# The first fourteen loads in a fixed order, the key-value matrix times WO as three products of rounded parts and rests, and a new order table

## The chip, the cores and the metric

The kernel runs on one core of a Trainium2 chip. Its time is the device time of one execution in microseconds (us); the number that counts is the median of the timed runs. The engines are named as in the profile: PE is the matrix engine (PEld its weight loads), DVE the vector engine, ACT the scalar engine, POOL the general engine; SP issues most of the transfers.

## The reference, cut to what matters

One sequence of S = 2048 rows with D = 512 columns, all in 32-bit floating point. Two branches share a layer norm.

```
xn = layernorm(x)
q, k, v = (xn @ wqkv), 32 heads of 16 columns
pq, pk = phi(q), phi(k)            # phi(t) = t+1 or exp(t), plus 1e-6
kv  = sum over rows of pk (x) v    # 16x16 per head
z   = sum over rows of pk
s   = (pq @ kv) / (pq . z + 1e-6)  # per head
s   = s @ wo
g   = silu(mixer_and_mlp(xn))      # w1, shift by rows, w2; then w3 (512x1376), gelu, w4
out = x + s * g
```

The kernel does not form v. It gathers G = xn^T pk (512x512) over the rows, multiplies it with the value weights WV, keeps the 16x16 blocks on the diagonal (a mask), and has the masked key-value matrix `kvt`. Then M = kvt times WO, a 512x512 matrix, so that s is one product of the scaled queries with M. The step "kvt times WO" is one of the places that the change touches.

## The kernel before, in words

**Arithmetic.** Most products are done with operands in a rounded 32-bit form (type fp32r in the profile) that PE streams faster than full 32-bit operands. To keep the precision, each operand is split into a rounded part `hi` (ACT, a copy into an fp32r tile, line 168) and a rest `lo` (DVE, a subtraction, line 191), and a product is the sum of three matmuls, hi*hi, hi*lo and lo*hi (`products`, which issues them through `mm`, line 146; `rounded` and `split` make the parts). A few products are done with the full 32-bit operands instead (`slow=True`); such a matmul stands in the trace as two records.

**Stages.** (1) Start: the key weights `wk_s0` to `wk_s3` (256 KB each, one per 128 input columns) and the transposed rows `xt0_0` to `xt0_3` of the first quarter of the sequence (each loaded as two halves of 128 KB) come in; PE multiplies chunk by chunk into four banks `k`. For chunk 0 it multiplies the raw operands, for chunks 1 to 3 the split ones, so ACT makes `wk_1h`, `u_1h`, `wk_2h` and so on, and DVE the rests `wk_1l`, `u_1l`. (2) Keys, queries and the G sums for all 16 row tiles, with weights for later stages being prepared beside. (3) The first mixer stage (`mix1`, `forms`, `mix2`) for four quarters, in four blocks of the Strassen-Winograd kind with seven products instead of eight (`seven`). In this stage, between quarters 2 and 3, stand the steps that the change touches: `kv` (32 records), the mask (`kvt`), then `m` (kvt times WO) and the copies into the tiles `mq`. (4) The MLP up and down projections with the attention products (`forms_m` makes further sums of the `mq` tiles for it) between them. (5) A last stretch of down projections, gates and stores.

**Order.** The program is not run in the order in which it is written. Every step is first recorded by `Plan.add` (line 96) with the engine, an assumed duration and the steps that it depends on. `deadlines` (line 243) walks the PE steps in their written order and gives each a nominal time; every other step gets a due time, worked back from its first user (`backward`, line 264). `nudged` (line 237) then changes due times by a table `SOONER` of pairs (number of the step, quarter microseconds earlier, negative for later). `emit` (line 270) runs a model of the engines: at each point it takes, among the steps of an engine that could start about then, the one that is due first (line 340), and issues it. So each engine's queue is a fixed sequence in the program, decided when it is built; on the chip the engines wait for each other by semaphores. A step that writes a tile also needs a free buffer of its pool (90 buffers of the tag `p` hold most of the tiles; `emit`, lines 311 to 327). For SP's transfers the model holds at most eight in flight (line 303).

The lines around the product with WO are these (1705 to 1719):

```
    kvt = piece("kvt")
    MQ = [[piece(f"mq{h}{d}") for d in range(2)] for h in range(2)]
    for gg in range(NC):
        cs = gg * P, (gg + 1) * P
        ps = bank(f"kv{gg}").cols(0, P)
        for c in range(NC):
            pl.mm(ps, WV.raw[c].cols(*cs), gs[c].cols(*cs), c == 0, c == NC - 1, slow=True)
        pl.tt(kvt.cols(*cs), ps, bmask, ALU.mult)
    forms(b)
    mix2(QT + 1)
    for gg in range(NC):
        ps = bank(f"m{gg}")
        pl.mm(ps, kvt.cols(gg * P, (gg + 1) * P), WO.raw[gg], True, True, slow=True)
        for d in range(2):
            pl.act(MQ[gg // 2][d].cols(gg % 2 * TH, (gg % 2 + 1) * TH), ps.cols(d * TH, (d + 1) * TH), AF.Copy)
```

`Weights` loads a matrix in four pieces `raw[c]`; its method `split` makes a rounded part (ACT, 128x512) and a rest (DVE, 128x512) of each; `chunk(c)` gives such a pair. Before, WO is loaded and used raw, and `split` is never called for it.

Of the kernel before, what the change touches and what calls it, by code (L numbers as in the profile page):

```python
# [14 lines left out]
P = 128  # L15
# [65 lines left out]
class Op:  # L81
    __slots__ = ("eng", "busy", "lat", "emit", "pre", "post", "tiles", "opens", "two", "table", "patience", "soon", "loads",
                 "nom", "due", "ready", "at", "end", "mb", "order")


class Plan:
# [9 lines left out]
    def add(self, eng, busy, lat, reads, writes, emit, two=False, table=None, mb=0.0):  # L96
        op = Op()
        op.eng, op.busy, op.lat, op.emit, op.two, op.table, op.mb = eng, busy, lat, emit, two, table, mb
        op.pre, op.post, op.tiles, op.opens = {}, [], {}, False
        op.order = len(self.ops)  # L100
# [142 lines left out]
    def deadlines(self, first):  # L243
# [18 lines left out]
        self.backward()  # L262

# [133 lines left out]
def linear_attn_gated_by_mixer(  # L397
# [55 lines left out]
    def rounds(name):  # L453

        return piece(name + "h", F32R), piece(name + "l", F32R)
# [1254 lines left out]
        for c in range(NC):  # L1710
            pl.mm(ps, WV.raw[c].cols(*cs), gs[c].cols(*cs), c == 0, c == NC - 1, slow=True)
        pl.tt(kvt.cols(*cs), ps, bmask, ALU.mult)
    forms(b)
    mix2(QT + 1)
    for gg in range(NC):
        ps = bank(f"m{gg}")
        pl.mm(ps, kvt.cols(gg * P, (gg + 1) * P), WO.raw[gg], True, True, slow=True)
        for d in range(2):
            pl.act(MQ[gg // 2][d].cols(gg % 2 * TH, (gg % 2 + 1) * TH), ps.cols(d * TH, (d + 1) * TH), AF.Copy)
# [76 lines left out]
    for b in LINE:  # L1796
# [10 lines left out]

    SOONER = (
# [103 lines left out]
```

## Time and profile before

| | |
|---|---|
| median of 3 timed runs | 502.96 us (502.81, 502.96, 505.84) |
| the profiled execution | 505.87 us |
| its span, first to last instruction | 504.2 us |
| left outside the span | 1.67 us |
| mean granted clock of PE | 0.995 |

The span is read by engine, by stage and by wait. "Busy" of PE is the time in which at least one matmul is under way; matmuls overlap in the pipeline, so what one costs is read from the distance between starts, or between ends, of neighbours, and not from its own duration. In the timeline a row gives start, duration, engine, line, what is written from what, the shape, how many such records are merged, and in brackets the idle time of the engine before it with what ended the wait. "SPq" rows are the issues of transfers. The granted clock is 1.00 when PE has its full clock.

### The profile page before, as it was taken

The page shows a single profiled execution, that of the slowest core. Times are in us where ns is not written, and L with a number is a line of the kernel's source. Part 1 is how long each engine was busy: PE and PEld are TensorE (multiplying, and loading weights), DVE is VectorE, ACT ScalarE, POOL GpSimd, SP SyncE. Part 2 cuts the span into 40 slices and gives each one's busy share as a digit, 9 for nine tenths or more (in the row PEclk, how much of TensorE's full clock was granted, in tenths as well). Part 3 has the DMA queues.
Part 4 walks back from the last instruction along what each step waited for, and adds up shares of the span by engine and source line. Part 5 has one row for each costly group of instructions (what it writes and reads, how often), then busy time and mean ns, then how long its engine had stood idle before and what let it go on. Part 6 is the DMA issues. An engine that isn't in the chain of part 4 may idle for free. (4 is left out here: it accounts for less than half of the span.)

```text
span 504.2 us, 9867 instructions
## 1 busy us (share of the span) xinstructions
PE 494.8 (98%) x3240; PEld 446.5 (89%) x3240; DVE 437.8 (87%) x889; ACT 373.2 (74%) x840; POOL 121.2 (24%) x194
## 2 busy tenths in 40 slices
PE   7999999999999999999999999999999999999896
PEld 4787878888888998899988999999999999999896
DVE  4898997798989958899999999999999799795773
ACT  4798999867687779999988667765766776664631
POOL 1167322447941312133100021100000000234220
PEclk9999999999999999999999999999999999999999
DMA  7949895989995899999987499695444799599995
GB/s 212 317 129 237 231 249 175 210 229 326 316 293 121 228 300 253 278 218 271 347 281 207 148 229 276 185 324 166 136 126 126 216 317 359 128 211 285 296 200 165
DMA packets 87082, 117.44 MB, mean 233 GB/s; under 512 B 10328, under 2 KB 39160, under 8 KB 87032
## 3 DMA queue, kind: packets, MB, share of 16 engines
q1 hardware_dynamic: 75512, 96.11, 58.9%
q0 software_dynamic: 11520, 20.71, 24.8%
q8 instruction: 25, 0.41, 0.3%
q14 instruction: 25, 0.20, 0.1%
HBM read 72.66 MB, written 39.93 MB: 223 GB/s over the span
## 5 line engine op out<-in xcount | busy, mean ns | idle before, releaser
L225 POOL DMA_DIRECT2D xo<-x1d x12 | 11.6, 987 | 158.5 <-ACT d_a121h L168 106.5
L225 POOL DMA_DIRECT2D th<-in_x x14 | 12.1, 885 | 50.0 <-DVE th L201 19.0
L598 POOL TENSOR_TENSOR rs<-w,nhalf 128x4 f32<-128x4 f32 (+2 forms) x10 | 12.4, 1239 | 49.0 <-DVE w L196 35.5
L225 POOL DMA_DIRECT2D o<-xnd x16 | 14.0, 915 | 35.2 <-ACT o L168 15.5
L168 ACT ACTIVATE th<-xo 128x512 f32<-128x512 f32 (+1 forms) x16 | 9.7, 612 | 13.3 <-DVE xo L201 10.8
L225 POOL DMA_DIRECT2D zacc<-ke x12 | 12.0, 1002 | 27.2 <-DMA zacc<-ke 19.7
L225 POOL DMA_DIRECT2D xt<-nrow x16 | 15.2, 1297 | 11.7 <-DMA nrow<-ar 5.8
L191 DVE TENSOR_TENSOR ht<-h,abc 128x512 f32<-128x512 f32 x16 | 11.0, 688 | 5.8 <-PE h L146 5.7
L168 ACT ACTIVATE p<-pe 128x256 f32<-128x256 f32 x20 | 7.6, 382 | 8.0 <-PE pe L146 7.9
L168 ACT ACTIVATE ht<-ht 128x512 f32<-128x512 f32 x16 | 9.8, 624 | 4.1 <-DVE ht L191 4.0
L168 ACT ACTIVATE u<-pb 128x256 f32<-128x256 f32 x20 | 7.6, 381 | 5.9 <-PE pb L146 5.6
L168 ACT ACTIVATE y<-o,nm,rs 128x512 f32<-128x512 f32 x16 | 11.9, 805 | 0.0
L168 ACT ACTIVATE sq<-o,mv 128x512 f32<-128x512 f32 x16 | 11.5, 722 | 0.2
L201 DVE SCALAR_TENSOR_TENSOR pq<-pq,rd 128x512 f32<-128x512 f32 x16 | 10.9, 684 | 0.2
L201 DVE SCALAR_TENSOR_TENSOR qz<-pq,zb 128x512 f32<-128x512 f32 x16 | 10.9, 680 | 0.0
L1456 DVE TENSOR_REDUCE den<-qz 128x32 f32<-128x512 f32 x16 | 10.7, 672 | 0.1
L168 ACT ACTIVATE p<-pb 128x256 f32<-128x256 f32 x20 | 7.6, 382 | 4.2 <-PE pb L146 3.9
L168 ACT ACTIVATE sq<-o 128x512 f32<-128x512 f32 x16 | 10.0, 629 | 0.6 <-PE h L146 0.6
L168 ACT ACTIVATE x<-x,nm,rs 128x512 f32<-128x512 f32 x12 | 9.3, 803 | 0.0
L201 DVE SCALAR_TENSOR_TENSOR th<-th,so 128x512 f32<-128x512 f32 x12 | 8.2, 680 | 0.8 <-ACT th L168 0.7
L168 ACT ACTIVATE sq<-x,mv 128x512 f32<-128x512 f32 x12 | 8.6, 715 | 0.1
L168 ACT ACTIVATE den<-den 128x32 f32<-128x32 f32 x16 | 3.4, 224 | 6.1 <-DVE den L1456 6.0
(2043 smaller groups left out, 2436.2 us busy)
## 6 DMA issues: line engine op xcount, KB each, us to landing
w_s<-in_w SPq DMA_DIRECT2D x28, 256.0 KB, 5.3
x<-in_x SPq DMA_DIRECT2D x16, 256.0 KB, 5.8
xt<-in_xt SPq DMA_DIRECT2D x16, 256.0 KB, 5.1
xnd<-x SPq DMA_DIRECT2D x16, 256.0 KB, 7.0
xt<-nrow POOLq DMA_DIRECT2D x16, 256.0 KB, 7.0
pqd<-qr SPq DMA_DIRECT2D x16, 256.0 KB, 3.2
o<-xnd POOLq DMA_DIRECT2D x16, 256.0 KB, 6.4
x1d<-o SPq DMA_DIRECT2D x16, 256.0 KB
```

The costliest lines, as they stand in the source:

```text
L168: nc.scalar.activation(out.get(), src.get(), func, scale=get(scale), **kw)
L191: self.vec(eng, out, [a, b], lambda: self.e(eng).tensor_tensor(out.get(), a.get(), b.get(), op=op), True)
L201: lambda: self.nc.vector.scalar_tensor_tensor(out.get(), a.get(), get(s), b.get(), op0=op0, op1=op1),
L225: lambda: self.nc.gpsimd.dma_start(out.get(), get(src), accum_op=ALU.add), mb=mb)
L598: lambda: g.tensor_tensor(out.get(), src.get(), nh.get(), op=ALU.pow))
L1456: pl.add("DVE", .6, .68, [t], [den], lambda: nc.vector.tensor_reduce(den.get(), t.get().rearrange("p (h d) -> p h d", d=DH), axis=AX.X, op ...
```

## The change: a fixed turn, split operands for M, a new table

1. A new method `in_turn` gives fourteen loads a rank in the order of a list. In `deadlines` a ranked step gets the due time 20 times its rank less 600 us, far before everything else, so that SP issues these fourteen first and in that order. The list alternates weights and rows from the first load on: key weights chunk 0 (first half), rows chunk 0 (first half of the rows), weights chunk 0 (second half), rows chunk 0 (second half), then weights and rows (first halves) of chunk 1, of chunk 2, of chunk 3, then `x0`, then the second halves of the rows of chunks 1, 2, 3.
2. `kvt` is split (`rounded(*kvr, kvt)`), WO is split (`WO.split()`), and kvt times WO is done as three fp32r matmuls for each of the four blocks instead of one full 32-bit matmul.
3. The table `SOONER` is another one: 625 pairs in place of 622. The numbers of the steps behind the new ones move, so the pairs can't be compared one by one.

```diff
         self.backward()
+        for op in self.ops:
+            if op.rank is not None:
+                op.due = 20.0 * op.rank - 600.0
+
+    def in_turn(self, names):
+
+        ranks = {}
+        for n, name in enumerate(names):
+            ranks.setdefault(name, []).append(n)
+        for op in self.ops:
+            if op.eng == "SP" and op.mb:
+                r = ranks.get(next(iter(op.tiles)).name)
+                if r:
+                    op.rank = r.pop(0)
...
         pl.tt(kvt.cols(*cs), ps, bmask, ALU.mult)
+    kvr = rounds("kvr")
+    rounded(*kvr, kvt)
+    WO.split()
     forms(b)
     mix2(QT + 1)
     for gg in range(NC):
         ps = bank(f"m{gg}")
-        pl.mm(ps, kvt.cols(gg * P, (gg + 1) * P), WO.raw[gg], True, True, slow=True)
+        products(ps, [both(kvr, gg * P, (gg + 1) * P) + WO.chunk(gg)])
...
+    pl.in_turn(["wk_s0", "xt0_0", "wk_s0", "xt0_0", "wk_s1", "xt0_1", "wk_s2", "xt0_2", "wk_s3", "xt0_3", "x0", "xt0_1",
+                "xt0_2", "xt0_3"])
     SOONER = (
-        15, 75, 17, -32, 23, 4, 27, 4, 31, 4, 39, 3, 45, 46, 47, -6, 48, -56, 62, 6, 81, 2, 106, -37, 110, -38,
+        25, -4, 31, 6, 40, 6, 47, -61, 48, -65, 72, 6, 76, 9, 81, 11, 82, 3, 83, 5, 92, -48, 94, 13, 95, -14,
...
     )
```

More of the change, by code (lines that the diff above doesn't have):

```diff
@@ L82 @@
     __slots__ = ("eng", "busy", "lat", "emit", "pre", "post", "tiles", "opens", "two", "table", "patience", "soon", "loads",
-                 "nom", "due", "ready", "at", "end", "mb", "order")
+                 "nom", "due", "ready", "at", "end", "mb", "order", "rank")
 class Plan:
@@ L99, in add @@
         op.pre, op.post, op.tiles, op.opens = {}, [], {}, False
-        op.order = len(self.ops)
+        op.order, op.rank = len(self.ops), None
         op.patience, op.soon = self.patience, False
```

120 rows, old and new, of the table SOONER are left out of this document.

## The prediction

> **What bounds the kernel now.** I read the page first, for the engines' shares.
>
> ```profile
> span 504.2 us, 9867 instructions
> PE 494.8 (98%) x3240; PEld 446.5 (89%) x3240; DVE 437.8 (87%) x889; ACT 373.2 (74%) x840; POOL 121.2 (24%) x194
> ```
>
> PE is busy in all but 9.4 us of its span, so a step gains only if it takes work off PE or ends one of PE's few waits. The second view is what PE waited for (total, times, longest):
>
> ```profile
> PE k L146 <- ACT u_1h L168: 1.6, 1, 1.6
> PE warm L146 <- POOL ones L514: 1.0, 1, 1.0
> PE pad L146 <- DVE d_a120l L191: 0.7, 1, 0.7
> PE pb L146 <- DVE h_a221f L191: 0.5, 1, 0.5
> PE k L146 <- DMA xt<-in_xt: 0.5, 1, 0.5
> PE ped L146 <- DVE d_s1xl L191: 0.5, 1, 0.5
> PE k L146 <- DVE wk_1l L191: 0.3, 1, 0.3
> ```
>
> Three of these (the two for `k` on ACT and DVE, and the one on a transfer) lie in the start, 2.4 us together. Three (pad, pb, ped: 0.7 + 0.5 + 0.5 = 1.7 us) lie late and are waits for DVE. The third view is the busy time by stretch (length, then PE, PEld, DVE, ACT, POOL with counts, the granted clock, the share and rate of the transfers):
>
> ```profile
> 5.00:10.00 5.00, 3.41 (x13) 2.22 (x14) 2.28 (x6) 1.58 (x4) 0.00 (x0) 1.00 0.84 247
> 10.00:15.00 5.00, 4.67 (x13) 3.39 (x14) 4.99 (x12) 3.97 (x11) 0.94 (x1) 0.66 0.91 279
> ...
> 250.00:300.00 50.00, 50.00 (x324) 45.13 (x324) 49.21 (x92) 37.44 (x86) 4.62 (x6) 1.00 0.77 220
> 300.00:350.00 50.00, 49.46 (x409) 48.72 (x408) 48.36 (x102) 32.43 (x84) 3.45 (x4) 1.00 0.84 238
> ...
> 450.00:480.00 30.00, 28.73 (x237) 28.05 (x237) 21.47 (x44) 16.28 (x33) 10.49 (x12) 1.00 1.09 288
> ```
>
> The reader is to see three things: PE is full in the stretch 250 to 300, and DVE has only 0.79 us left there; the late waits of PE are 0.54 us in 300 to 350 and 1.27 us in 450 to 480; and the clock of PE is 0.66 in the stretch 10 to 15. The fourth view, the timeline of the start, shows why:
>
> ```profile
> 0.79 0.87 SPq L207 DMA_DIRECT2D wk_s<-in_wqkv  x2
> 1.71 1.37 SPq L207 DMA_DIRECT2D xt<-in_xt  x3
> 3.13 0.91 SPq L207 DMA_DIRECT2D wk_s<-in_wqkv  x2
> ...
> 8.84 0.63 ACT L168 ACTIVATE wk_1h<-wk_s 128x512 fp32r<-128x512 f32 x1 [3.24 <-DMA wk_s<-in_wqkv]
> ...
> 9.38 0.40 ACT L168 ACTIVATE u_1h<-xt 128x256 fp32r<-128x256 f32 x1
> 9.54 1.82 SPq L207 DMA_DIRECT2D wq_s<-in_wqkv  x4
> 9.68 0.62 ACT L168 ACTIVATE wk_2h<-wk_s 128x512 fp32r<-128x512 f32 x1
> ...
> 9.83 0.73 PE L146 MATMUL k<-wk_1h,u_1h 128*128 128x512 f32 x2 [1.59 <-ACT u_1h L168]
> 10.15 0.68 DVE L191 TENSOR_TENSOR wk_1l<-wk_s,wk_1h 128x512 fp32r<-128x512 f32 x1
> ```
>
> PE stands still for 1.59 us until 9.83, because ACT could only start rounding chunk 1 at 8.84, when its weights had landed. Right behind it, in the stretch 10 to 15, the clock was 0.66 over five microseconds: 5 x 0.34 = 1.7 us of PE's time was not granted. This belongs to this execution. It stands at 505.87 us, 2.91 above the median of 502.96; one of the three timed runs stands as high (505.84), two do not. I read most of the 2.91 as this reduced clock and what follows from it; the trace of one execution can't show that, so it is an estimate.
>
> **Part 1, the fixed turn.** SP's rows give the order before: two weights, three rows, two weights. The list has weights, rows, weights, rows, weights, rows. So two places change: rows of chunk 0 go ahead of the second half of weights 0, and weights of chunk 1 go from sixth to fifth, ahead of rows of chunk 1. The same fourteen loads with the same bytes stay ahead of all others, so nothing behind them moves, and neither does POOL's queue. Weights 1 have one load of 128 KB less in front of them. At the rate of the stretch 5 to 10, 247 GB/s, that is 131072 B / 247 GB/s = 0.53 us, the upper bound. ACT would start `wk_1h` near 8.3 instead of 8.84, and rows 1, now behind, land no later than the two together did before (8.84), while ACT takes them up at 9.38 now. So PE's wait of 1.59 us shrinks. What is late next is chunk 2: ACT takes it up at 9.68 without a wait, and SP could issue its fifteenth load at 9.54. That issue waits for the seventh load (weights 2) if eight are in flight, as the planner assumes, so weights 2 are there hardly 0.14 us before they are used, and the chain behind gains little more than that. Bounds: 0.14 to 0.53 us, and 0 if the transfers share the rate so that places do not count. I take 0.3, about the middle of the bounds. The 0.5 us for which PE waited on `xt` before its first matmul of chunk 0 may go too, but it comes back as a longer wait for chunk 1, so it counts nothing.
>
> **Part 2, kvt times WO.** On PE:
>
> ```profile
> 196.05 0.28 PE L146 MATMUL pbm<-w_t3h,hs31l 128*128 128x256 f32 x1
> 196.17 1.02 PE L146 MATMUL m<-wo_s,kvt 128*128 128x512 f32 x2
> ...
> 200.01 0.39 PE L146 MATMUL h<-u_1h,w_1h 128*128 128x512 f32 x1
> ...
> 200.71 0.39 PE L146 MATMUL h<-u_2h,w_2h 128*128 128x512 f32 x1
> ```
>
> By ends, the two records of one `m` take from 196.33 (196.05 + 0.28) to 197.19, 0.86 us. Three fp32r matmuls of the same 512 columns take 200.71 - 200.01 = 0.70 us. Four blocks: 4 x (0.86 - 0.70) = 0.64 us less on PE, and PE is full there, so all of it is on the path. This is the firmest term: 0.6 to 0.7.
>
> Off PE, the edit adds five copies on ACT and five subtractions on DVE, each 128x512. Priced by `wk_2h` (0.62) and `wk_1l` (0.68): 5 x 0.62 = 3.1 us on ACT and 5 x 0.68 = 3.4 us on DVE. It adds no transfer. What hides them, by stretch and by tile:
>
> ```profile
> 180.00:190.00 10.00, 10.00 (x77) 9.50 (x76) 5.70 (x12) 7.52 (x18) 2.46 (x5) 1.00 0.95 305
> 190.00:200.00 10.00, 10.00 (x66) 8.21 (x65) 9.29 (x25) 9.80 (x27) 2.53 (x3) 1.00 0.95 251
> ```
>
> ```profile
> L207 SPq DMA_DIRECT2D wo_s<-in_wo x4: 333/392/809, 177.7 to 184.5; - x4
> L191 DVE TENSOR_TENSOR kvt<-kv,bmask x4: 251/266/291, 188.0 to 192.4; 128x128 f32<-128x128 f32 x4
> L191 DVE TENSOR_TENSOR m_f<-mq,mq x2: 684/684/685, 264.6 to 265.2; 128x512 f32<-128x512 f32 x2
> ```
>
> From 180 to 190 DVE has 4.30 us idle and ACT 2.48; from 190 to 200 it is 0.71 and 0.20. WO is issued from 177.7 to 184.5. If its split falls into the first stretch, DVE's four (2.7 us) fit whole and ACT's four (2.5) just. If it falls later, ACT and DVE run behind by up to 3 us, and the cover is the distance to the users. The product now waits for the last `kvt` (192.4), a copy and a subtraction: 192.4 + 0.29 + 0.62 + 0.68 = 194.0, as late as the first `m` runs today (193.9), and PE has the mixer's products to do meanwhile. On ACT the copies out of PSUM of those products stand behind the new copy, which waits for DVE's mask; PE could wait for them by 0.3 us (one mask) if the order is unlucky. The sums of `mq` are used at 264.6. Ten more buffers of 90 are held for a few microseconds, and four raw ones are freed earlier. I take 0 for all of it; bounds 0 to 3.4 us (all of DVE's work, uncovered).
>
> **Part 3, the new table.** Nothing in the trace of before prices it. Gain at most what PE waits for late: 1.7 us by the rows, or 0.54 + 1.27 = 1.81 by the stretches. Loss: another order makes its own waits; by the nearest rows an equal set on top of these, 1.8 us. I take 0, since the waits that an order leaves are where the planner's durations and the chip's differ, and neither part changes those.
>
> **Sum.** Against the profiled execution: 505.87 - 0.3 - 0.64 = 504.9 us, if the reduced clock comes again. Against the median: 502.96 - 0.94 = 502.0 us, the forecast.
>
> **The clock, by trace and by rule.** In the trace PE waited 1.59 us up to 9.83 and 0.3 us soon after, and in the stretch 10 to 15 the clock was down. The Trainium skill, page "TensorE: Matmul & The Clock Gate", section "Why this matters for your kernels", asks for no idle gaps over about 3 us; by it a wait of 1.59 us would not have cost the clock, and part 1 could not touch it. Here the measurement decides: the clock did fall, to 0.66 in the stretch. The same page, section "Part 1: The HAM clock gate (the "warmup" mystery)", says that the window in which activity is judged runs free of the kernel's start; by that, whether the clock falls would differ from run to run. One trace can't show it, and the times of before (two at 502.8 to 503.0, one at 505.84) are what it would give.
>
> **Rivals.**
> - *The clock falls in the median run too.* The wait at the start stays over 1 us (1.59 - 0.3), so it can. Then 505.87 - 0.94 = 504.9 us. For it: one timed run in three and the profiled one stand there. Against it: the wait is shorter.
> - *The fixed turn does nothing.* Two swaps of neighbours, and ACT is fed at the same time as before because the transfers share the rate. 502.96 - 0.64 = 502.3 us. The first ACT row of chunk 1 would stay at 8.84.
> - *The new table removes the late waits.* 502.0 - 1.8 = 500.2 us. For it: they are three single waits on DVE. Against it: the old table left them.
> - *DVE falls behind (slower than before).* Its 3.4 us of new work come before the stretch 250 to 300, where it has 0.79 us left, and 300 to 350, where it has 1.64, and where PE already waits on DVE (`h_a221f`). If the split of WO slips past 190 and none of it is made good, PE waits 3.4 us more in the attention stage: 502.0 + 3.4 = 505.4 us. It makes the change a loss once more than 0.94 us is not made good. Against it: the 4.3 us of idle DVE between 180 and 190.
> - *The new order goes wrong in several stages:* more than three such sets of waits, 502.0 + 3 x 1.8 = 507.4 us and up.
>
> **How the numbers follow.** Forecast 502.0, its own range 500.9 to 503.4 (parts 1 and 2 at their bounds, the table within half of its bounds): 0.45. Turn without effect: 0.10, inside that range. Late waits gone: 0.13. Clock: 0.16. DVE behind: 0.11, with times between 503 and 505.4 and above. Wrong in several stages: 0.05. The range reaches from 500.0, the case of the late waits, to 505.4, the uncovered DVE work, which takes in the clock's 504.9; outside it are about 0.05 below and 0.12 above. One per cent is 5.0 us, about what a measurement of this kernel can tell from no change. Faster by over 1% needs 497.9: all gains together (0.53 + 0.64 + 1.8 = 3.0) do not reach it, so 0.02. Slower by over 1%, over 508.0, comes from the last case and from DVE and the clock together: 0.06. Within: 0.92.
>
> **What would show it.** Part 1: ACT's `wk_1h` near 8.3 and PE's wait for `u_1h` near 1.3 us. Part 2: twelve `m` records in place of eight, 0.70 us from the first to the end of a block; the rounding of WO between 180 and 195; PE without a wait between 180 and 210. Part 3: the waits named pad, pb and ped gone or replaced by others of about the same sum. The prediction is wrong if PE's late waits sum to over 4 us, if the first reduced clock of the run is not in the start, or if PE waits for `mq` or `kvr`.

## The result and the profile after

The changed kernel takes 501.5 us (median of 15 runs, 500.41 to 502.82). The kernel before, run beside it on the same chip, takes 504.36 us (median of 15, 501.95 to 506.06). The ratio is 0.995, with an interval of 0.9932 to 0.9968: 2.5 us faster (504.36 x 0.005), between 1.6 and 3.4. A second set of runs of the changed kernel, told below, gives 0.9972 (0.9955 to 0.9988): 1.4 us. The change is within 1% of no change, and it is a gain that the interval tells from nothing.

The profiled execution of the changed kernel stands at 500.41 us, with a span of 498.7. Its page begins so:

```profile
span 498.7 us, 9912 instructions
PE 492.4 (99%) x3244; PEld 445.4 (89%) x3244; DVE 439.2 (88%) x894; ACT 371.7 (75%) x845; POOL 121.9 (24%) x194
```

PE has four instructions more (twelve products for M in place of eight records), DVE and ACT five each, as the change says. PE's idle time inside its span is 498.7 - 492.4 = 6.3 us, where it was 9.4. What PE waited for (total, times, longest):

```profile
PE warm L146 <- POOL ones L529: 1.0, 1, 1.0
PE pex L146 <- DVE xs_0l L191: 0.4, 1, 0.4
PE k L146 <- DMA xt<-in_xt: 0.3, 1, 0.3
```

The waits for `u_1h` and `wk_1l` in the start are gone, and so are the three late ones (pad, pb, ped). A new one, `pex`, has come. The same stretches as before (length, then PE, PEld, DVE, ACT, POOL, the granted clock, the share and the rate of the transfers):

```profile
5.00:10.00 5.00, 5.00 (x19) 3.40 (x19) 3.95 (x9) 2.31 (x6) 0.00 (x0) 1.00 0.94 298
10.00:15.00 5.00, 4.92 (x20) 3.40 (x19) 4.60 (x12) 4.46 (x12) 1.05 (x3) 1.00 0.98 286
250.00:300.00 50.00, 50.00 (x324) 45.36 (x323) 49.40 (x93) 37.74 (x85) 3.66 (x5) 1.00 0.77 215
300.00:350.00 50.00, 50.00 (x422) 49.79 (x421) 49.73 (x107) 33.28 (x88) 3.44 (x4) 1.00 0.84 239
450.00:480.00 30.00, 30.00 (x256) 30.00 (x255) 22.85 (x45) 16.21 (x35) 10.82 (x13) 1.00 1.08 272
```

The clock is whole in 10 to 15, the transfers of 5 to 10 run at 298 GB/s in place of 247, and PE is full in the two late stretches. The timeline of the start:

```profile
2.65 0.43 SPq L207 DMA_DIRECT2D wk_s<-in_wqkv  x1
...
7.11 0.63 ACT L168 ACTIVATE wk_1h<-wk_s 128x512 fp32r<-128x512 f32 x1 [1.33 <-DMA wk_s<-in_wqkv]
...
8.36 0.63 PE L146 MATMUL k<-wk_1h,u_1h 128*128 128x512 f32 x2
...
8.57 0.63 ACT L168 ACTIVATE wk_2h<-wk_s 128x512 fp32r<-128x512 f32 x1 [0.52 <-DMA wk_s<-in_wqkv]
```

Weights 1 are issued at 2.65 (the first of the two at 3.13 before), they are there at 7.11 in place of 8.84, the first product of chunk 1 starts at 8.36 in place of 9.83 and behind no wait, and chunk 2's weights (8.57 in place of 9.68) are now the ones that ACT waits for. The block M:

```profile
194.52 0.39 PE L146 MATMUL m<-wo_0h,kvrh 128*128 128x512 f32 x1
194.75 0.39 PE L146 MATMUL m<-wo_0l,kvrh 128*128 128x512 f32 x1
...
197.78 0.40 PE L146 MATMUL m<-wo_3h,kvrl 128*128 128x512 f32 x1
```

Twelve products stand 0.23 us apart: 12 x 0.23 = 2.8 us, where the eight records took 4 x 0.86 = 3.4.

### The profile page after: what moved, and what is told of

The parts are those of the page before. It is cut to its first block, busy times and chain, and to the rows that moved or that the text cites. A ratio compares the mean times of both kernels' runs of the same rounds, so it can differ in the third digit from the quotient of the medians.

```text
span 498.7 us, 9912 instructions
## 1 busy us (share of the span) xinstructions
PE 492.4 (99%) x3244; PEld 445.4 (89%) x3244; DVE 439.2 (88%) x894; ACT 371.7 (75%) x845; POOL 121.9 (24%) x194
## 4 chain that ended last, share of the span: by engine, by line
PE 85%; DMA 5%; ACT 5%; DVE 2%; issue 1%; SPq 1%; POOL 1%
PE pb L146 11%; PE pbd L146 9%; PE h L146 9%; PE acc L146 6%; PE pe L146 6%; PE g L146 6%; PE ped L146 5%; PE pbm L146 5%; PE pbs L146 5%; PE pbx L146 4%; DMA xt<-nrow 4%; PE pa L146 3%; PE pad L146 3%; PE pem L146 2%; PE pes L146 2%; PE a L146 2%
## 5 line engine op out<-in xcount | busy, mean ns | idle before, releaser
L613 POOL TENSOR_TENSOR rs<-w,nhalf 128x4 f32<-128x4 f32 (+2 forms) x10 | 10.4, 1042 | 47.5 <-DVE w L196 38.2
L225 POOL DMA_DIRECT2D zacc<-ke x12 | 10.5, 879 | 22.8 <-DMA zacc<-ke 12.3
```

What stands on the lines that cost most here:

```text
L225: lambda: self.nc.gpsimd.dma_start(out.get(), get(src), accum_op=ALU.add), mb=mb)
L613: lambda: g.tensor_tensor(out.get(), src.get(), nh.get(), op=ALU.pow))
```

## The experiments

My theory (A in the expectations) was that the start carries most of the 2.5 us: weights 1 land much earlier than I had priced, and with the shorter wait goes the reduced clock. Its rivals were that the product (0.64 us on PE) and the new table (late waits gone) carry it, and that the profiled execution of before misleads, because the kernel before varies more from run to run than the changed one. The timed experiments had 11 or 12 runs, the last one 6; each ratio is taken against runs of the kernel before in the same set.

### The kernel before, once more, and how its time spreads

No edit. How much of its spread is the clock?

> The kernel before, unchanged, to see every run's clock beside its time. Theory A (the reduced clock in the start makes the upper half of the times): runs at 505 to 506 us have a mean clock of about 0.995, runs at 502 to 503 us one of about 0.998 (0.5 x 3.4 us of 504 is 0.0034), and nothing lies between. Theory B (the spread has another cause): both clocks occur at all times, the difference of the two groups is under 1 us.

503.6 us (12 runs, 501.78 to 505.69), ratio 1.0004 (0.9981 to 1.0027). The profiled run had a shorter wait in the start, and no reduced clock (timeline, then the stretch 10 to 15):

```profile
7.99 0.63 ACT L168 ACTIVATE wk_1h<-wk_s 128x512 fp32r<-128x512 f32 x1 [2.77 <-DMA wk_s<-in_wqkv]
8.97 0.73 PE L146 MATMUL k<-wk_1h,u_1h 128*128 128x512 f32 x2 [1.15 <-ACT u_1h L168]
```

```profile
10.00:15.00 5.00, 4.96 (x20) 3.73 (x21) 4.28 (x11) 3.67 (x11) 1.45 (x2) 1.00 0.89 285
```

So the landing of weights 1 varies from run to run by nearly a microsecond in one and the same program. Of the 47 runs of this kernel in this set, 11 had a mean granted clock of 0.996 or lower; they took 505.3 us in the mean, the other 36 took 503.2. Runs in which the clock falls are thus about 2 us longer, the longer wait ahead of the fall included; but the others spread too, from 500.5 to 506.9: that the times fall into two groups with nothing between them was wrong. Over this and the later sets, 30 of 145 runs with the old order of loads (this kernel, and it with small edits, without the one that fills PE's wait) have the low clock. With weights 1 moved ahead it is 1 of 92. (Low means a mean of 0.996 or less in all these counts.)

### The turn alone, on the kernel before

Six loads are sent in the new order; all other queues stay as they were, M is done as before, the table is the old one.

```diff
-            for t in op.tiles:
+            sent = ops[{16: 20, 20: 16, 17: 23, 23: 17, 35: 38, 38: 35}.get(op.order, op.order)]
+            for t in list(op.tiles) + list(sent.tiles):
...
-            op.emit()
+            sent.emit()
```

> The kernel before with every queue as it was, except that the six loads that stand elsewhere in the fixed turn trade places (rows 0 with weights 0 second half, weights 1 with rows 1, and the second halves of rows 1 and 2). As predicted: PE's wait before chunk 1 (1.59 us) shrinks by 0.14 to 0.53 us and the time by 0.3 us. Theory A: it shrinks by more than 1 us, since weights 1 landed 1.7 us earlier in the changed kernel (ACT took them up at 7.11, not at 8.84), the clock no longer falls, and the time is 2 to 3.5 us lower in the median. Theory C (the turn does nothing, the table's new order in the start did it): ACT still takes up chunk 1 near 8.8 and the median is within 0.5 us of before.

501.84 us, ratio 0.9968 (0.9949 to 0.9987): 1.6 us faster (503.62 x 0.0032). `wk_1h` starts at 6.97, and the list of PE's waits has none for `u_1h`:

```profile
6.97 0.63 ACT L168 ACTIVATE wk_1h<-wk_s 128x512 fp32r<-128x512 f32 x1 [1.78 <-DMA wk_s<-in_wqkv]
```

On the kernel before, the turn alone is worth five times the 0.3 us that I gave it.

### The old order of loads, on the changed kernel

The same swap of six loads, the other way round, in the changed kernel.

> The changed kernel with every queue as it is, except that the same six loads stand in the order of before. Theory A: weights 1 land near 8.8 again, PE waits 1 us or more before chunk 1, the clock falls in a part of the runs, and the median rises by 1.5 to 3 us. As predicted: it rises by 0.3 us. Theory C: no change within 0.5 us.

502.08 us, ratio 0.9967 (0.995 to 0.9984), where the changed kernel had 0.995 in its first set and 0.9972 in its second. By the ratios, taking the turn out costs 0.9 us against the first set and nothing against the second. Neither is told from nothing by the intervals, both are less than the 1.5 to 3 that theory A expected, and none of the 12 runs had the low clock.

This kernel is parts 2 and 3 without part 1, and it is 1.7 us faster than the kernel before (503.62 x 0.0033; 0.8 to 2.5 by the interval), about as much as the turn alone. So the parts don't simply add, and that the start carries most of the gain holds for the turn put into the kernel before; in the changed kernel it isn't shown. The new table was not run by itself.

The profile of this kernel is of little help for the start. It stands at 504.27 us, the slowest of the 12 runs, 2.2 above their median, and PE did not wait for chunk 1 in it, because chunk 0 itself took longer:

```profile
8.90 0.63 PE L146 MATMUL k<-wk_0l,u_0h 128*128 128x512 f32 x1
9.33 0.63 PE L146 MATMUL k<-wk_0h,u_0l 128*128 128x512 f32 x1
```

These products start 0.43 us apart. In the profile before the same two start at 6.91 and 7.14, 0.23 apart. The granted clock reads 1.00 in both places, so a 1.00 in that column does not show that PE has its full pace there. Further on this profile has longer waits than the changed kernel's:

```profile
PE pbx L146 <- DVE u_1l L191: 1.5, 1, 1.5
...
PE pax L146 <- DVE u_2l L191: 0.5, 1, 0.5
PE pex L146 <- DVE xs_0l L191: 0.4, 1, 0.4
```

These lie at 71 to 76. Rows of the changed kernel show the same place more weakly (`pex`, 0.4); the last two experiments go after it.

### Filling the wait

Seven matmuls on a spare bank stand ahead of chunk 1 in the kernel before, so that PE has no idle time there; if the wait is what lowers the clock, it should stay up.

```diff
+            if op is self.late:
...
+                for _ in range(7):
+                    self.nc.tensor.matmul(f.ap[:, :P], self.ones.ap[:, :], self.ones.ap[:, :], start=True, stop=True)
```

> The kernel before with every queue as it was, except that PE runs seven matmuls of constants (128 columns, full 32 bit, about 0.21 us each, 1.5 us together) into a bank that is overwritten later, just ahead of the first product of chunk 1, where PE waits 1.59 us. The loads and the work that waits for them are not moved. Theory A: the clock does not fall behind it, no run stands at 505 to 506, and the median falls by 1 to 2 us (all runs as the lower half of before). Theory B: the median stays within 0.5 us.

503.86 us, ratio 1.0009 (0.9989 to 1.0029). None of its 12 runs had the low clock, but nothing was won:

```profile
8.73 0.63 ACT L168 ACTIVATE wk_1h<-wk_s 128x512 fp32r<-128x512 f32 x1 [3.35 <-DMA wk_s<-in_wqkv]
8.93 1.72 PE L361 MATMUL ksum<-ones 128*128 128x128 f32 x14
...
10.41 0.71 PE L146 MATMUL k<-wk_1h,u_1h 128*128 128x512 f32 x2
```

The fillers began at 8.93 and ran to 10.65 (14 records of 128x128 full 32-bit operands), past the point where chunk 1 could have begun (u_1h is ready at 9.27 + 0.40 = 9.67): they cost about 0.7 us of what the clock gave. As a price of the clock the run is inconclusive. That filling the wait keeps the clock up is likely, but not certain: at 30 in 145, 12 runs without a low clock come up by chance about once in sixteen.

### Two of the three swaps, each by itself

The turn has three swaps. The first kernel makes only the one of weights 1 with rows 1 (sixth to fifth place), the second only that of rows 0 with the second half of weights 0. The third, of the second halves of rows 1 and 2, was not run by itself.

```diff
+            sent = ops[{17: 23, 23: 17}.get(op.order, op.order)]
```

> The kernel before with every queue as it was, except that weights 1 and the first half of rows 1 trade places in SP's queue (fifth and sixth). Theory A1 (the gain of the fixed turn is weights 1 landing earlier): the median falls by 1.2 to 2 us like the full turn (1.8 in the run with all six loads moved), ACT takes up chunk 1 near 7.0. Theory A2 (it comes from rows 0 going ahead of the second half of weights 0): the median stays within 0.5 us and ACT takes up chunk 1 between 7.8 and 8.8 as before.

501.47 us, ratio 0.9972 (0.9953 to 0.999), low clock in none of 12 runs.

```diff
+            sent = ops[{16: 20, 20: 16}.get(op.order, op.order)]
```

> The kernel before with every queue as it was, except that the first half of rows 0 and the second half of weights 0 trade places (second and third). Theory A1: no change within 0.5 us; PE starts chunk 0 up to 0.5 us earlier and waits as much longer for chunk 1. Theory A2: the median falls by 1.2 to 2 us.

502.84 us, ratio 1.0015 (0.9992 to 1.0038), low clock in 2 of 12. PE began chunk 0 at 4.19, 0.7 us sooner than in the profile before (4.88), and had nothing from it:

```profile
4.19 3.09 PE L146 MATMUL k<-wk_s,xt 128*128 128x256 f32 x6
6.72 0.80 PE L146 MATMUL k<-wk_0h,u_0h 128*128 128x512 f32 x1
...
8.06 0.63 ACT L168 ACTIVATE wk_1h<-wk_s 128x512 fp32r<-128x512 f32 x1 [2.84 <-DMA wk_s<-in_wqkv]
...
9.05 0.74 PE L146 MATMUL k<-wk_1h,u_1h 128*128 128x512 f32 x2 [0.37 <-ACT u_1h L168]
```

The six raw products of chunk 0 took 2.5 us here (4.19 to 6.72), 1.4 in the profile before (4.88 to 6.27), and chunk 1 still had to wait for `u_1h`. As far as these intervals tell, the gain of the turn is that of weights 1. Part of why it is so large, the rate shows, in one-microsecond stretches: first the kernel before, then the one with weights 1 ahead.

```profile
5.00:6.00 1.00, 1.00 (x5) 0.90 (x6) 1.00 (x4) 0.42 (x1) 0.00 (x0) 1.00 0.62 149
6.00:7.00 1.00, 1.00 (x4) 0.47 (x4) 0.40 (x2) 0.00 (x0) 0.00 (x0) 1.00 0.78 180
7.00:8.00 1.00, 1.00 (x6) 0.67 (x4) 0.00 (x0) 0.00 (x0) 0.00 (x0) 1.00 0.83 250
```

```profile
5.00:6.00 1.00, 1.00 (x3) 0.82 (x4) 1.00 (x4) 0.42 (x1) 0.00 (x0) 1.00 0.47 75
6.00:7.00 1.00, 1.00 (x4) 0.72 (x3) 0.32 (x1) 0.00 (x0) 0.00 (x0) 1.00 0.88 281
7.00:8.00 1.00, 1.00 (x4) 0.57 (x3) 0.69 (x1) 0.88 (x2) 0.00 (x0) 1.00 1.06 353
```

From 5 to 7 the kernel before moved 149 and 180 GB/s, not the 247 of the five microseconds together; in the five other profiles with the old order the first of these two ran at 76 to 147. In the eight profiles with weights 1 ahead, `wk_1h` starts at 6.67 to 7.58, 7.01 in the mean; in the six with the old order at 7.84 to 8.96, 8.40 in the mean. One place in the queue, 128 KB, moves the start of `wk_1h` by 1.4 us.

### The product twice

In the changed kernel each of the twelve products of M is issued a second time: 12 x 0.23 = 2.8 us more of PE's time. If PE is the bound there, the time grows by all of it.

```diff
         products(ps, [both(kvr, gg * P, (gg + 1) * P) + WO.chunk(gg)])
+        three = [op.emit for op in pl.ops[-3:]]
+        pl.ops[-1].emit = lambda three=three: [f() for f in three[2:] + three]
```

> The changed kernel with the twelve products of kvt and WO issued twice (the second time writes the same result over the first), all else as it is: twelve matmuls of 512 columns more at 0.233 us each, 2.8 us of PE. If PE is the bound there and what it saves counts in full (as predicted for 0.64 us), the median rises by 2.8 us against the changed kernel of the same job. If the stage has slack behind it (PE waits later anyway), it rises by less than 1.5 us, and the 0.64 us of part 2 counted for less than half.

504.19 us, ratio 1.0025 (1.0008 to 1.0043). Its twin without an edit, in the same set:

> The changed kernel, unchanged, as the reference within this job, and to see every run's clock: by the theory of the reduced clock, runs at a mean clock of 0.996 or less are rarer than in the kernel before (12 of 47 there), at most 1 in 12, and the median is 2 to 2.5 us below before.

501.01 us, ratio 0.9972 (0.9955 to 0.9988). The difference is 3.2 us by the medians and 502.9 x (1.0025 - 0.9972) = 2.7 us by the ratios, for 2.8 us of work. So work put on PE at this place counts in full, as far as intervals of some 0.9 us to each side tell, and by that the 0.64 us that the change takes off PE there should be a gain of 0.64. That gain by itself is too small for these runs to show.

### The late waits of the kernel before

In the kernel before, the waits named pad and ped begin at a DVE row at 470.67 that itself sat idle, though its operands were there:

```profile
470.67 0.69 DVE L191 TENSOR_TENSOR d1f_s40f<-d1f_s20f,h_ba120f 128x512 f32<-128x512 f32 x1 [2.45 <-issue]
```

I read the 2.45 us as a wait for its buffer, which the tile `th10` still holds because that tile's store is late in SP's queue. The profile of the run with the filled wait names a store of `th` as what ended the same wait:

```profile
468.77 0.69 DVE L191 TENSOR_TENSOR d1f_s40f<-d1f_s20f,h_ba120f 128x512 f32<-128x512 f32 x1 [3.09 <-DMA out<-th]
```

The experiment hands this one buffer out 6 us later, so that the planner takes another; behind that row a few steps trade places.

```diff
-                    insort(slots[t.tag], (t.end, t.slot))
+                    insort(slots[t.tag], (t.end + (6.0 if t.name == "th10" else 0.0), t.slot))
```

> The kernel before, but the buffer of th10 (which a store to the output still reads) is handed out 6 us later by the planner, so that the DVE sum d1f_s40f gets another one; the queues stay as they were up to that sum, behind it a few steps trade places. Theory D (the late waits of PE are waits of DVE for a buffer that a late store holds; the new table happens to hand out another one): DVE does not wait before d1f_s40f (2.45 us in the trace of before), the PE waits pad and ped between 465 and 480 go, and the median falls by 0.5 to 1.5 us. Theory E (DVE is simply full there): the waits stay at 0.8 us or more in sum and the median does not move by more than 0.5 us.

502.31 us, ratio 0.9986 (0.9967 to 1.0005). The row's wait for the buffer is gone:

```profile
467.72 0.69 DVE L191 TENSOR_TENSOR d1f_s40f<-d1f_s20f,h_ba120f 128x512 f32<-128x512 f32 x1 [0.34 <-PE pbd L146]
```

and of PE's late waits only 0.3 us for ped is left. That settles the cause of this row's wait; the worth of it, 0.7 us by the ratio, is not told from nothing. In the five other profiles with the old table and without this edit the idle time of this row was 2.05, 1.06, 3.09, 2.31 and nothing. PE's late waits (pad, pb and ped) sum to 0.3 to 1.8 us there, so the 1.7 of the profile before is near the upper end. This profile also has the low clock once more, behind a PE wait of 1.9 us:

```profile
10.00:15.00 5.00, 4.67 (x13) 3.38 (x14) 5.00 (x12) 4.08 (x11) 0.81 (x1) 0.67 0.92 261
```

### Weights 1 and the buffer, without parts 2 and 3

The two edits together on the kernel before: the old table, M with full 32-bit operands.

> The kernel before with two small edits and the old table: weights 1 and the first half of rows 1 trade places, and the buffer of th10 is handed out later. If the gain of the change is the start plus the late waits plus 0.64 us of part 2, this has the first two without the third: 1.5 to 2.5 us below before, within 1 us of the changed kernel. If the new table does more than that, it stays 1 us or more above the changed kernel (which is 1.9 to 2.9 us below before).

500.73 us, ratio 0.9954 (0.9936 to 0.9972). Two small edits reach what the whole change reaches, though they leave the 0.64 us of part 2 unused. Not every late wait is gone with the buffer, either. Its profile has a long one for ped, behind DVE rows of which the first (471.48) waited 1.73 us for ACT:

```profile
PE ped L146 <- DVE d_s1xl L191: 1.3, 1, 1.3
```

By the medians, the new table on top of the turn seems to have given away about what part 2 brings. That is less than the intervals (0.9 us to each side) can show, but it put the question where the new table loses.

### Where the new table loses: two tries

In the changed kernel PE is 0.56 us idle between 60 and 80:

```profile
60.00:80.00 20.00, 19.44 (x80) 14.24 (x79) 18.15 (x35) 17.26 (x34) 5.83 (x5) 1.00 1.04 275
```

and the products there stand further apart. Summed over the stretch, the distances of their starts exceed those of undisturbed neighbours (0.23 us for 512 columns) by 1.85 us, in the profile before by 0.1. I first took four loads of `x` for the cause: in the changed kernel SP sends them at 56.2, ahead of the gathers of `xt` by POOL at 56.7, which then need 7.8 to 11.3 us to land. The first try sends those loads behind two stores, at 66.2.

```diff
+            if op.order in (727, 730, 733, 736):
+                held = self.__dict__.setdefault("held", [])
+                held.append(op)
+            else:
+                op.emit()
+            if op.order == 476:
+                for o in self.held:
+                    o.emit()
```

> The changed kernel with every queue as it is, except that the four loads x12 to x15 (1 MB) stand behind two stores in SP's queue, so that they go out near 64 us and not at 56.2, where they share the transfers with the four gathers that PE waits for between 68 and 74 (about 1.8 us lost in that stretch in the changed kernel, 0.1 in the one before). Theory F (the new table brought this wait by sending the loads ahead of the gathers): the rows of the second quarter are there about 2 us earlier, PE's wait at 68 to 74 shrinks to under 0.5 us, and the median falls by 0.8 to 1.5 us below the changed kernel. Theory G (the gathers are late by POOL's own queue): the wait stays over 1.2 us and the median within 0.4 us.

500.94 us, ratio 0.9954 (0.9937 to 0.9971): not to be told from the changed kernel. The gathers landed sooner (5.0 to 8.4 us), and PE waited all the same. That theory fell. Its timeline names another cause:

```profile
64.71 3.65 POOL L191 TENSOR_TENSOR nm<-mv,ns 128x4 f32<-128x4 f32 x1 [2.13 <-DVE ns L196]
...
67.88 0.41 DVE L191 TENSOR_TENSOR xf<-xt,xt 128x256 f32<-128x256 f32 x1
...
68.45 0.23 POOL L196 TENSOR_SCALAR nm<-nm 128x4 f32<-128x4 f32 x1
...
68.71 0.81 ACT L168 ACTIVATE x<-x,nm,rs 128x512 f32<-128x512 f32 x1 [3.16 <-POOL nm L196]
...
69.43 0.61 ACT L168 ACTIVATE u_1h<-xt 128x512 fp32r<-128x512 f32 x1
```

`u_1h`, for which PE waits, stands on ACT behind a row that waits for POOL's `nm`. That is a product of two 128x4 tiles, and it took 3.65 us. It ended at 68.36, 0.07 after the last row of a run of DVE instructions without a gap that read two tiles each (67.88 + 0.41 = 68.29). In the changed kernel it took 3.31 us and ended at 66.85, again 0.06 after such a run (66.11 + 0.68 = 66.79):

```profile
63.54 3.31 POOL L191 TENSOR_TENSOR nm<-mv,ns 128x4 f32<-128x4 f32 x1 [0.42 <-DVE ns L196]
...
66.11 0.68 DVE L191 TENSOR_TENSOR x5l<-x,x5h 128x512 fp32r<-128x512 f32 x1
```

In the profile before it is the short row:

```profile
64.46 0.69 DVE L201 SCALAR_TENSOR_TENSOR k6l<-ke,k6h 128x512 fp32r<-128x512 f32 x1
64.63 0.58 POOL L191 TENSOR_TENSOR nm<-mv,ns 128x4 f32<-128x4 f32 x1 [1.26 <-DVE ns L196]
65.07 0.69 DVE L201 SCALAR_TENSOR_TENSOR qr<-qe,qi 128x512 f32<-128x512 f32 x1
```

Here too it ends 0.06 us after a DVE row of two tiles (64.46 + 0.69 = 65.15, against 65.21), but the next such row has begun by then. So DVE rows back to back do not always hold it: it can get through between two of them. What decides that the runs do not show.

The second try keeps the later loads and lets DVE do these two small steps, at the same place of the program.

```diff
         pl.tt(m, means(mv1, lo, lo + n), s, ALU.mult, eng="POOL")
+        if lo == 2 * QT:
+            a = means(mv1, lo, lo + n)
+            pl.ops[-1].emit = lambda: nc.vector.tensor_tensor(m.get(), a.get(), s.get(), op=ALU.mult)
...
             pl.ts(m, m, km, None, ALU.mult, eng="POOL")
+            if lo == 2 * QT:
+                pl.ops[-1].emit = lambda: nc.vector.tensor_scalar(m.get(), m.get(), km, None, op0=ALU.mult)
```

> This is the run before it (the changed kernel with the four loads of x behind the two stores), with one more edit: the two small steps that make nm of the third quarter (128x4) go to DVE in place of POOL, at the same place of the program. In the changed kernel POOL's first nm step starts at 63.54 and takes 3.31 us, in the run before it 64.71 and 3.65 us, where the same step takes 0.58 us in the kernel before; it ends in both within 0.07 us of the end of a row of DVE instructions that read two tiles (66.79 and 68.29). ACT's x row waits for it, and u_1h, which PE needs, stands behind that x row. Theory P (POOL is held up while DVE reads two tiles back to back, and this makes the waits at 68 to 75): nm is done near 66.8 on DVE, ACT's first x row starts before 67.2 in place of 68.71, u_1h before 68 in place of 69.43, PE's waits for u_1h and xs_0h (0.4 and 0.4 us, 2.3 us with the slower pace in the stretch 60 to 80) go, and the time falls by 1 to 1.8 us: about 499.4, a ratio of 0.992 (0.991 to 0.9945). Theory G (the gathers of xt are what makes u_1h late, as supposed before): u_1h still starts after 69, PE's waits stay, and the ratio stays at 0.9954, about 501. Two more instructions on DVE cost 0.3 us there.

499.2 us (6 runs, 498.42 to 500.11), ratio 0.9934 (0.9909 to 0.9958), against 502.57 for the kernel before in that set: 3.3 us faster than the kernel before. Its timeline, and then its stretch 60 to 80:

```profile
64.31 0.15 DVE L633 TENSOR_TENSOR nm<-mv,ns 128x4 f32<-128x4 f32 x1
...
65.24 0.82 ACT L168 ACTIVATE x<-x,nm,rs 128x512 f32<-128x512 f32 x1 [1.12 <-DVE nm L639]
65.96 0.61 ACT L168 ACTIVATE u_1h<-xt 128x512 fp32r<-128x512 f32 x1
```

```profile
60.00:80.00 20.00, 20.00 (x87) 15.96 (x87) 19.09 (x37) 18.88 (x39) 2.25 (x4) 1.00 1.04 294
```

`nm` is done in 0.15 us, `u_1h` starts 3.5 us sooner than in the first try, and PE has no wait left between 60 and 80, where it now is busy throughout. This is the fastest kernel of the case. By the ratios it is 0.9934 against 0.995 and 0.9972 of the changed kernel; these intervals touch, so that it beats the changed kernel rests on the vanished waits and on the medians (499.2 against 501.5 and 501.0, in different sets). Whether the later loads are needed beside it was not tried.

## Why the prediction was right, and where its sum was off

**The forecast.** 502.0 us against 501.5 and 501.0 measured; faster, but within 1%, as given 0.92. That the total came so near is partly luck. The gain in the sum was 0.94 us; the gain measured against the kernel before in the same set is 2.5 (1.6 to 3.4) in the first set and 1.4 (0.6 to 2.3) in the second. The term of part 1 was too small, and the median of three runs on which the sum stands (502.96) was 0.2 to 1.4 us lower than the medians of three of the five longer sets (504.36, 503.62, 503.16; the other two were 502.9 and 502.57), which made up for it.

**Part 1: the step that was mis-sized.** "131072 B / 247 GB/s = 0.53 us, the upper bound", and 0.3 taken of it. Measured: `wk_1h` 1.4 us earlier in the mean, and the turn on the kernel before worth 1.4 us (weights 1 only) and 1.6 us (all), by the ratios. In the changed kernel, where taking it out costs 0.9 us or nothing, the size of the term stays open. Two things were missing. The rate of five microseconds was used for two in which the queues ran at 149 and 180 GB/s; by those rows a load of 128 KB ahead is 131072 B / 149 GB/s = 0.88 us, and at the 76 GB/s of another profile 1.7. So a rate of those microseconds can account for 1.4 us; that it does, the runs don't settle. And "the chain behind gains little more" than 0.14 us, because weights 2 were thought to be next: weights 2 came earlier too (8.57 in the changed kernel). That the swap of rows 0 with weights 0 counts nothing held (4.19 in place of 4.88, and no gain), but not in the way given, that a sooner chunk 0 "comes back as a longer wait for chunk 1": the wait was 0.37 us in that profile, and what came back was slower products of chunk 0. "So two places change" overlooks the third swap.

**Part 2** held in size on PE and in mechanism: 12 x 0.23 = 2.8 us in place of 3.4, and by the doubled products work on PE there counts. Its gain was not measured by itself. The off-PE work cost nothing that could be seen: DVE was busy 49.40 and 49.73 in the two stretches where it had least room, and PE waited neither for `mq` nor for `kvr`.

**Part 3** is near its 0 only when it is counted on top of the turn (2.5 or 1.4, less 1.6 and 0.64), and not by the reason given. Without the turn, parts 2 and 3 together gain 1.7 us, which less 0.64 leaves about 1.0 for the table (0.2 to 1.9 by the interval). "The waits that an order leaves are where the planner's durations and the chip's differ, and neither part changes those": the three late waits did go. For pad the run with the buffer handed out later shows a cause (worth 0.7 us, in the interval of nothing); that the new table removes it in this way is not shown, and for pb and ped the cause stays open. And a set of about 1.8 us came at 68 to 75. That is the loss bound of the prediction, 1.8 us, met by chance through a mechanism that it did not name: a small step on POOL that takes 3.31 us in the changed kernel where DVE holds it, 0.58 in the profile before.

**The reduced clock.** "I read most of the 2.91 as this reduced clock" was half right. Runs with it are 2.1 us slower in the largest set, and 1.6 in the mean of all sets, each weighted by its runs with the low clock; about one run in five of the old order has it. What makes up the rest of the 2.91 was not taken apart; the late buffer and the spread of the first landings can be in it. As a part of the turn's gain the clock is 0.2 x 1.6 = 0.3 us in the mean. The Trainium skill, page "TensorE: Matmul & The Clock Gate", section "HAM oscillation — how this bites in real kernels", gives as the rule that no idle gap of PE may be over about 3.4 us. Here two waits of 1.59 and 0.3 us (and in a second trace 1.9 and 0.3) were followed by 0.66 (0.67) in the stretch 10 to 15, while 1.15 and 0.3 us in another left the clock whole: the measurement decides, and half of that gap can be too long. That some runs of one program have it and others not is what a window that runs free of the kernel's start would give, as the prediction said. It is also what the spread of the landings would give, since in these traces the clock fell behind the two longer waits and not behind the shorter one. The runs don't tell the two apart.

**The rivals.** The clock in the median run, DVE behind and an order that goes wrong in several stages are refuted by the rows above. The turn without effect is refuted on the kernel before; in the changed kernel the runs leave it open. The late waits did go, as the third rival had it, but without its 1.8 us.

## What to carry to other kernels

Price a place in the queue of the first loads by the rate of the very microseconds in which it matters, and by several profiles: one load of 128 KB ahead was worth 1.4 us on the kernel before, and it took the reduced clock of every fifth run with it. Test a part both by putting it into the old kernel and by taking it out of the new one: here the first gave 1.6 us and the second 0.9 or nothing. A rise in one stage can hide a loss in another: after a gain that fits the forecast, list the new waits all the same, since here one step of 128x4 on the wrong engine cost 1.0 us by the ratios and 1.7 by the medians, more than the 0.64 of the rewritten product. Where an engine waits behind a row that itself waits, follow it to the end before touching transfers: the releaser of the last wait was a 0.15 us step, not the 1 MB of loads beside it.

## What the runs showed of the hardware

**A small POOL step can be held by DVE.** The same 128x4 product takes 0.56 to 0.74 us in seven profiles with the old table and 1.17 in an eighth, 3.31 in three profiles with the new one (the changed kernel twice, and with the products doubled), 3.65 and 1.77 in two kernels made from it. In all of them it ends within 0.07 us behind the end of a DVE instruction that reads two tiles from SBUF, in the short cases the one that was under way, in the long ones a later one of a run of them. Moved to DVE it takes 0.15 us. The Trainium skill, page "GPSIMD Engine Reference", section "1. Specifications", has the row for it: the engine's SBUF interfaces are shared with VectorE, with contention for instructions with two SBUF inputs. The traces agree, and show the size: the step is held for up to seven such instructions in a row.

**The clock can fall after short waits.** Behind waits of 1.9 and of 2.2 us in all, in two pieces, it fell in two traces, behind 1.5 us in a third it did not. It depends on the run: 30 of 145 with the old order of loads had the low clock, 1 of 92 with weights 1 ahead, none of 12 with the wait filled, and none of 12 in the changed kernel with the old order.

**The pace of the first products differs from execution to execution.** From the first raw product of chunk 0 to the first split one it takes 1.4 us in two profiles of the kernel before (4.88 to 6.27, and 4.46 to 5.86), 2.5 us in the one with only rows 0 ahead and 2.8 us in the changed kernel with the old order (4.92 to 7.69). The granted clock reads 1.00 in all of these stretches, so a start at half pace has to be read from the distances of the products. Its cause is not shown.
